# Seven block products in place of eight in a two-layer expert network, with the instruction order made by a list scheduler

## The chip, the cores and the metric

The kernel runs on one core of a Trainium2 chip. Times are device microseconds from the first to the last work of an execution. Every run is marked fast or slow; medians below name which runs they cover. "PE" is TensorE's matrix unit, "PEld" its weight load, "DVE" VectorE, "ACT" ScalarE, "POOL" GpSimd, "SP" SyncE, which here issues DMAs.

## The reference, cut to what matters

```python
# linear attention: batch 8, heads 8, seq 576, head_dim 64
q_p, k_p = phi(q), phi(k)                  # phi(x) = elu(x) + 1
kv = einsum('bhsd,bhse->bhde', k_p, v);  z = sum(k_p, over s)
x  = (q_p @ kv) / (q_p @ z + 1e-6)         # reshaped to 4608 tokens x 512
# mixture of 4 experts, all of them for every token
p = domain_probs / sum(domain_probs)
for e in range(4):
    h = maximum(x @ w1[e], 0)              # 512 -> 1024
    out += p[:, e] * (h @ w2[e])           # 1024 -> 512
```

The expert network is nearly all of the arithmetic: 4608 tokens, 4 experts, two products of 512 x 1024.

## The kernel before

It keeps all weights in SBUF as fp16 and goes through tokens in nine tiles of 512. For each tile and expert (a "unit" of 64 matmuls) it makes the first layer, ACT applies the ReLU while it moves PSUM to SBUF, then the second layer, and DVE multiplies by p and adds to a sum in SBUF. The attention of later batches is emitted between the tiles.

```python
def emit_unit(j, e):                       # 512 tokens, one expert
    for fj in range(FC):                   # 8
        for dc in range(DC):               # 4
            nc.tensor.matmul(out=ph, lhsT=w1_sb[e][:, dc, fj*P:(fj+1)*P],
                             rhs=xT_all[:, dc, j*NT:(j+1)*NT], ...)   # 512 columns
        nc.scalar.activation(ht, ph, AF.Relu)
    for ns in range(NSUB):                 # 4
        for fj in range(FC):               # 8
            nc.tensor.matmul(out=py, lhsT=hT[fj][:, ns*P:(ns+1)*P],
                             rhs=w2_sb[e][:, fj, :], ...)             # 512 columns
        nc.vector.scalar_tensor_tensor(out=acc[:, ns, :], in0=py, scalar=pscal,
                                       in1=acc[:, ns, :], op0=AO.mult, op1=AO.add)
# weights: fp32 by DMA (SP queue) into a staging tile, then a cast by DVE (w1) or ACT (w2)
# order at the start:
emit_attention_batch(0); emit_w1(0); emit_w2(0); emit_probs(); emit_w1(1)
emit_unit(0, 0); emit_attention_batch(1); emit_w2(1); emit_unit(0, 1)
# [...] weights of experts 2 and 3 between units of tiles 0 and 1, then tile after tile
```

Of the kernel before, what the change touches and what calls it, by code (L numbers as in the profile page):

```python
# [7 lines left out]


FP32 = mybir.dt.float32  # L10
# [4 lines left out]
SX = float(2.0**14)  # L15
INV = float(2.0 ** (-14))
# [3 lines left out]
def kernel(  # L20
# [10 lines left out]
    nc = tc.nc  # L31
# [6 lines left out]
    R = 96  # L38
    KC = S // R
    QC = S // (2 * R)  # L40
    HD = H * D
    DC = HD // P
    FC = F // P
    NT = 512
    NTILES = N // NT
    NSUB = NT // P
    DE = D + 1
    HG = 4
    NG = H // HG
    NCH = (S + P - 1) // P  # L50
    TAIL = S - (NCH - 1) * P
    NTP = N // P

    pconst = ctx.enter_context(tc.tile_pool(name="pconst", bufs=1))
    identh = pconst.tile([P, P], FP16, tag="identh")
    make_identity(nc, identh)
    NKV = 3
    kvs = []
    for i in range(NKV):
        kvz = pconst.tile([P, 2, DE], FP16, tag=f"kvz{i}", name=f"kvz{i}")  # L60
        nc.gpsimd.memset(kvz, 0.0)
        kvs.append(kvz)
    n_kv = [0]

    pw = ctx.enter_context(tc.tile_pool(name="pw", bufs=1))
    w1_sb = [pw.tile([P, DC, F], FP16, tag=f"w1_{e}", name=f"w1_{e}") for e in range(E)]
    w2_sb = [pw.tile([P, FC, Dm], FP16, tag=f"w2_{e}", name=f"w2_{e}") for e in range(E)]
    w1_src = moe_w1.rearrange("e (dc p) f -> e p dc f", p=P)
    w2_src = moe_w2.rearrange("e (fc p) d -> e p fc d", p=P)
    p_sb = pw.tile([P, NTP, E], FP32, tag="pnorm")  # L70

    px = ctx.enter_context(tc.tile_pool(name="px", bufs=1))
    xT_all = px.tile([P, DC, N], FP16, tag="xT")

    pa = ctx.enter_context(tc.tile_pool(name="pa", bufs=1))
    pm = ctx.enter_context(tc.tile_pool(name="pm", bufs=1))
    ppm = ctx.enter_context(tc.tile_pool(name="ppm", bufs=1, space=bass.MemoryType.PSUM))
    ppa = ctx.enter_context(tc.tile_pool(name="ppa", bufs=1, space=bass.MemoryType.PSUM))

    out_tiled = out.rearrange("(j ns p) d -> j p ns d", ns=NSUB, p=P)  # L80

    def emit_w1(e):
        FQ = F // 4
        for h4 in range(4):
            wr = pw.tile([P, DC, FQ], FP32, tag="wraw", bufs=3)
            nc.sync.dma_start(out=wr, in_=w1_src[e, :, :, h4 * FQ : (h4 + 1) * FQ])
            nc.vector.tensor_copy(w1_sb[e][:, :, h4 * FQ : (h4 + 1) * FQ], wr)

    def emit_w2(e):
        for h4 in range(4):  # L90
            wr = pw.tile([P, 2, Dm], FP32, tag="wraw", bufs=3)
            nc.sync.dma_start(out=wr, in_=w2_src[e, :, h4 * 2 : h4 * 2 + 2, :])
            nc.scalar.copy(w2_sb[e][:, h4 * 2 : h4 * 2 + 2, :], wr)  # L93

    def emit_probs():
        p_raw = pw.tile([P, NTP, E], FP32, tag="praw")
        nc.sync.dma_start(
            out=p_raw, in_=moe_domain_probs.rearrange("(nt p) e -> p nt e", p=P)
        )
        p_rsum = pw.tile([P, NTP], FP32, tag="prsum")  # L100
        nc.vector.tensor_reduce(
            out=p_rsum, in_=p_raw, axis=mybir.AxisListType.X, op=AO.add
        )
        nc.vector.tensor_scalar(p_rsum, p_rsum, 1e-9, None, AO.add)
        nc.vector.reciprocal(p_rsum, p_rsum)
        nc.vector.scalar_tensor_tensor(
            out=p_sb,
            in0=p_raw,
            scalar=INV,
            in1=p_rsum.broadcast_to([P, NTP, E]),  # L110
            op0=AO.mult,
            op1=AO.mult,
        )

    def emit_attention_batch(b):
        for g in range(NG):
            hs = slice(g * HG, (g + 1) * HG)
            kst = pa.tile([R, HG, KC, D], FP32, tag="kst", bufs=2)
            vst = pa.tile([R, HG, KC, D], FP32, tag="vst", bufs=2)
            qst = pa.tile([R, QC, HG, 2, D], FP32, tag="qst", bufs=2)  # L120
            nc.sync.dma_start(
                out=kst, in_=k[b, hs].rearrange("h (p c) d -> p h c d", p=R)
            )
            nc.sync.dma_start(
                out=vst, in_=v[b, hs].rearrange("h (p c) d -> p h c d", p=R)
            )
            q_src = q[b, hs].rearrange("h (c p r) d -> c p h r d", c=QC, r=2)
            for c in range(QC):
                nc.sync.dma_start(out=qst[:, c], in_=q_src[c])



            kp = pa.tile([R, KC, HG, D], FP16, tag="kp", bufs=2)
            kpv = kp.rearrange("p c h d -> p h c d")
            ek = pa.tile([R, HG, KC, D], FP16, tag="phie", bufs=2)
            nc.scalar.activation(ek, kst, AF.Exp)  # L136
            nc.vector.tensor_scalar(kpv, kst, 0.0, 1.0, AO.max, AO.add)
            nc.vector.tensor_tensor(out=kpv, in0=ek, in1=kpv, op=AO.min)

            vp = pa.tile([R, KC, HG, DE], FP16, tag="vp", bufs=2)  # L140
            nc.gpsimd.memset(vp[:, :, :, D:DE], 1.0 / SX)
            nc.scalar.copy(vp[:, :, :, 0:D].rearrange("p c h d -> p h c d"), vst)  # L142

            qp = pa.tile([R, QC, 2, HG, D], FP16, tag="qp", bufs=2)
            eq = pa.tile([R, QC, HG, 2, D], FP16, tag="phie", bufs=2)
            nc.scalar.activation(eq, qst, AF.Exp)  # L146
            for c in range(QC):
                qv = qp[:, c].rearrange("p r h d -> p h r d")
                nc.vector.tensor_scalar(qv, qst[:, c], 0.0, 1.0, AO.max, AO.add)
                nc.vector.tensor_tensor(out=qv, in0=eq[:, c], in1=qv, op=AO.min)  # L150

            for pr in range(HG // 2):
                h0 = pr * 2
                pair = g * (HG // 2) + pr
                psum_kv = ppa.tile([P, 2, DE], FP32, tag="aps", bufs=3)
                for c in range(KC):
                    nc.tensor.matmul(  # L157
                        out=psum_kv,
                        lhsT=kp[:, c, h0 : h0 + 2, :],
                        rhs=vp[:, c, h0 : h0 + 2, :],  # L160
                        start=(c == 0),
                        stop=(c == KC - 1),
                    )
                kvz = kvs[n_kv[0] % NKV]
                n_kv[0] += 1
                nc.scalar.copy(out=kvz[0:D, 0, :], in_=psum_kv[0:D, 0, :])
                nc.scalar.copy(out=kvz[D:P, 1, :], in_=psum_kv[D:P, 1, :])

                psum_qT = ppa.tile([P, QC, 2, R], FP16, tag="aps", bufs=3)
                for c in range(QC):  # L170
                    for r in range(2):
                        nc.tensor.transpose(  # L172
                            out=psum_qT[:, c, r, :],
                            in_=qp[:, c, r, h0 : h0 + 2, :],
                            identity=identh[0:R, 0:R],
                        )
                qT = pa.tile([P, S], FP16, tag="qTsb", bufs=2)
                nc.vector.tensor_copy(
                    out=qT, in_=psum_qT.rearrange("p c r i -> p (c r i)")
                )  # L180

                x_sb = pa.tile([P, NCH, 2, D], FP16, tag="xsb", bufs=2)
                for c0, c1 in ((0, 3), (3, NCH)):
                    psum_nd = ppa.tile([P, 3, 2, DE], FP32, tag="aps", bufs=3)
                    for c in range(c0, c1):
                        w = P if c < NCH - 1 else TAIL
                        nc.tensor.matmul(  # L187
                            out=psum_nd[0:w, c - c0],
                            lhsT=qT[:, c * P : c * P + w],
                            rhs=kvz,  # L190
                            start=True,
                            stop=True,
                        )
                    recip = pa.tile([P, 3, 2, 1], FP32, tag="recip", bufs=3)
                    for a0, a1, w in (
                        ((0, 3, P),) if c1 == 3 else ((0, 1, P), (1, 2, TAIL))
                    ):
                        nc.vector.reciprocal(
                            recip[0:w, a0:a1], psum_nd[0:w, a0:a1, :, D:DE]
                        )  # L200
# [8 lines left out]
                for c in range(NCH):  # L209
# [10 lines left out]
                    in_=psum_xT.rearrange("p (c r i) -> p c r i", c=QC, r=2),  # L220
                )

    accs = {}

    def emit_unit(j, e):
        if e == 0:
# [97 lines left out]
```

## Time and profile before

| before | value |
|---|---|
| time, median of the first 3 runs | 595.45 us |
| PE busy | 563.3 of 593.0 us |
| DVE, ACT busy | 234.2, 286.2 us |
| one group of 32 matmuls with 512 columns | 6.91 us, so 216 ns each |
| one tile of 512 tokens with a batch of attention | 62.31 us (from 188.37 to 250.68) |

The page of the kernel before: busy time of each engine, rows of the 40 slices of the span (a digit is tenths busy), and the chain of work that ended last.

```profile
span 593.0 us, 7743 instructions
PE 563.3 (95%) x3008; PEld 266.6 (45%) x3008; DVE 234.2 (39%) x516; ACT 286.2 (48%) x449; POOL 12.9 (2%) x25
...
PE   1789997999999999999999999999999999999997
...
DMA  9989889915556003800181010000100010000001
...
PE 82%; DMA 7%; ACT 6%; DVE 3%; issue 1%; SPq 0%; ACTq 0%
```

PE is busy for 70% or more of each slice from the second (a slice is 14.8 us) and for 90% or more from the eighth to the last but one, and the DMA engines are busy for 80% or more of each of the first eight slices, in which the weights and two batches arrive. From the chain in order of time (start, duration, what):

```profile
188.37 6.91 PE ph L233 x32
...
250.68 6.91 PE ph L233 x32
```

These are the first-layer matmuls of one expert in two successive tiles: 62.31 us from tile to tile. The timeline of PE around 136 us shows how narrow matmuls follow one another:

```profile
136.10 0.33 PE L211 MATMUL psum_xT<-identh,x_sb 128*128 128x128 f16 x3
...
136.38 0.45 PE L157 MATMUL psum_kv<-vp,kp 96*128 96x130 f16 x5
136.67 0.38 PE L233 MATMUL ph<-xT_all,w_3_75 128*128 128x512 f16 x1
```

Five matmuls of 130 columns, each with a weight load of its own, begin at 136.38 and the next group at 136.67: 58 ns apart. The change rests on such short matmuls.

### The profile page before, as it was taken

The page shows a single profiled execution, that of the slowest core. Times are in us where ns is not written, and L with a number is a line of the kernel's source. Part 1 is how long each engine was busy: PE and PEld are TensorE (multiplying, and loading weights), DVE is VectorE, ACT ScalarE, POOL GpSimd, SP SyncE. Part 2 cuts the span into 40 slices and gives each one's busy share as a digit, 9 for nine tenths or more (in the row PEclk, how much of TensorE's full clock was granted, in tenths as well). Part 3 has the DMA queues.
Part 4 walks back from the last instruction along what each step waited for, and adds up shares of the span by engine and source line. Part 5 has one row for each costly group of instructions (what it writes and reads, how often), then busy time and mean ns, then how long its engine had stood idle before and what let it go on. Part 6 is the DMA issues. An engine that isn't in the chain of part 4 may idle for free.

```text
span 593.0 us, 7743 instructions
## 1 busy us (share of the span) xinstructions
PE 563.3 (95%) x3008; PEld 266.6 (45%) x3008; DVE 234.2 (39%) x516; ACT 286.2 (48%) x449; POOL 12.9 (2%) x25
## 2 busy tenths in 40 slices
PE   1789997999999999999999999999999999999997
PEld 0434443445454445544454445444544444444443
DVE  3737733528466225722382228322522222222222
ACT  4476765738657334833394338333543333333332
POOL 0000000001000000000000001000000000000000
PEclk9979998999999999999999999999999999999999
DMA  9989889915556003800181010000100010000001
GB/s 214 258 255 297 236 274 273 261 28 129 183 155 156 1 0 101 211 1 1 72 197 43 1 55 19 1 0 23 50 0 2 1 72 0 1 36 35 1 1 71
DMA packets 54644, 55.09 MB, mean 93 GB/s; under 512 B 6992, under 2 KB 45904, under 8 KB 54608
## 3 DMA queue, kind: packets, MB, share of 16 engines
q1 hardware_dynamic: 54608, 54.61, 33.2%
q8 instruction: 23, 0.38, 0.3%
q14 instruction: 13, 0.11, 0.1%
HBM read 45.16 MB, written 9.44 MB: 92 GB/s over the span
## 4 chain that ended last, share of the span: by engine, by line
PE 82%; DMA 7%; ACT 6%; DVE 3%; issue 1%; SPq 0%; ACTq 0%
PE py L247 39%; PE ph L233 36%; DMA wr<-in_moe_w_dram 6%; PE psum_nd L187 2%; DMA kst<-in_k_dram 2%; PE psum_xT L211 2%; ACT ht L241 2%; PE psum_kv L157 2%; PE psum_qT L172 1%; ACT xT_all L216 1%; ACT ek L136 1%; ACT eq L146 1%; DVE x_sb L201 1%; DVE acc L258 0%; ACT w_1_77 L93 0%
## 5 line engine op out<-in xcount | busy, mean ns | idle before, releaser
L241 ACT ACTIVATE ht<-ph 128x512 f16<-128x512 f32 x288 | 168.4, 598 | 209.3 <-PE ph L233 208.9
L258 DVE SCALAR_TENSOR_TENSOR acc<-py,p_sb,acc 128x512 f32<-128x512 f32 x108 | 81.0, 750 | 263.4 <-PE py L247 263.4
L247 PEld LDWEIGHTS <-ht 128*128 128x128 f16 x1152 | 111.6, 98 | 133.3 <-issue 3.3
L233 PE MATMUL ph<-xT_all,w_0_72 128*128 128x512 f16 x288 | 78.1, 394 | 3.4 <-ACT xT_all L216 2.6
L233 PE MATMUL ph<-xT_all,w_1_73 128*128 128x512 f16 x288 | 64.9, 380 | 3.3 <-ACT ht L241 3.3
L247 PE MATMUL py<-w_0_76,ht 128*128 128x512 f16 x288 | 67.0, 379 | 0.1
L247 PE MATMUL py<-w_1_77,ht 128*128 128x512 f16 x288 | 66.6, 385 | 0.3 <-DVE acc L258 0.2
L233 PE MATMUL ph<-xT_all,w_3_75 128*128 128x512 f16 x288 | 64.9, 379 | 0.0
L247 PE MATMUL py<-w_3_79,ht 128*128 128x512 f16 x288 | 64.1, 379 | 0.0
L233 PE MATMUL ph<-xT_all,w_2_74 128*128 128x512 f16 x288 | 64.0, 379 | 0.1
L247 PE MATMUL py<-w_2_78,ht 128*128 128x512 f16 x288 | 63.7, 379 | 0.0
L233 PEld LDWEIGHTS <-w_1_73 128*128 128x128 f16 x288 | 27.9, 98 | 36.1 <-issue 3.6
L233 PEld LDWEIGHTS <-w_2_74 128*128 128x128 f16 x288 | 28.2, 98 | 34.4 <-issue 0.7
L256 DVE TENSOR_SCALAR acc<-py,p_sb 128x512 f32<-128x512 f32 x36 | 27.0, 749 | 39.0 <-PE py L247 39.0
L233 PEld LDWEIGHTS <-w_3_75 128*128 128x128 f16 x288 | 27.7, 98 | 32.6
L233 PEld LDWEIGHTS <-w_0_72 128*128 128x128 f16 x288 | 26.0, 100 | 28.2 <-issue 6.1
L201 DVE TENSOR_TENSOR x_sb<-psum_nd,recip 128x384 f16<-128x384 f32 (+2 forms) x96 | 32.7, 368 | 0.5
L157 PE MATMUL psum_kv<-vp,kp 96*128 96x130 f16 x192 | 18.9, 231 | 10.3 <-ACT vp L142 10.3
L216 ACT COPY xT_all<-psum_xT 128x576 f16<-128x576 f16 x32 | 25.7, 804 | 5.3 <-PE psum_xT L211 4.8
L146 ACT ACTIVATE eq<-qst 96x1536 f16<-96x1536 f32 x16 | 23.7, 1481 | 9.3 <-DVE qp L150 6.4
L136 ACT ACTIVATE ek<-kst 96x1536 f16<-96x1536 f32 x16 | 23.8, 1488 | 6.2 <-DMA kst<-in_k_dram 4.5
L142 ACT CAST vp<-vst 96x1536 f16<-96x1536 f32 x16 | 23.9, 1494 | 2.1 <-DMA vst<-in_v_dram 2.0
(44 smaller groups left out, 261.2 us busy)
## 6 DMA issues: line engine op xcount, KB each, us to landing
wr<-in_moe_w_dram SPq DMA_DIRECT2D x32, 512.0 KB, 5.2
kst<-in_k_dram SPq DMA_DIRECT2D x16, 576.0 KB, 5.5
vst<-in_v_dram SPq DMA_DIRECT2D x16, 576.0 KB, 6.7
qst<-in_q_dram SPq DMA_DIRECT2D x48, 192.0 KB, 5.2
out_dram<-acc SPq DMA_DIRECT2D x36, 256.0 KB, 2.0
p_raw<-in_moe_domain_probs_dram SPq DMA_DIRECT2D x1, 72.0 KB, 8.8
```

The lines of the kernel that those rows point to most:

```text
L136: nc.scalar.activation(ek, kst, AF.Exp)
L142: nc.scalar.copy(vp[:, :, :, 0:D].rearrange("p c h d -> p h c d"), vst)
L146: nc.scalar.activation(eq, qst, AF.Exp)
L157: nc.tensor.matmul(out=psum_kv, lhsT=kp[:, c, h0 : h0 + 2, :], rhs=vp[:, c, h0 : h0 + 2, :], start=(c == 0), stop=(c == KC - 1),)
L187: nc.tensor.matmul(out=psum_nd[0:w, c - c0], lhsT=qT[:, c * P : c * P + w], rhs=kvz, start=True, stop=True,)
L201: nc.vector.tensor_tensor(out=x_sb[0:w, c0 + a0 : c0 + a1], in0=psum_nd[0:w, a0:a1, :, 0:D], in1=recip[0:w, a0:a1].broadcast_to([w, a1 - a ...
L216: nc.scalar.copy(out=xT_all[:, pair, b * S : (b + 1) * S].rearrange("p (c i r) -> p c r i", c=QC, r=2), in_=psum_xT.rearrange("p (c r i) - ...
L233: nc.tensor.matmul(out=ph, lhsT=w1_sb[e][:, dc, fj * P : (fj + 1) * P], rhs=xT_all[:, dc, j * NT : (j + 1) * NT], start=(dc == 0), stop=(d ...
L241: nc.scalar.activation(ht, ph, AF.Relu)
L247: nc.tensor.matmul(out=py, lhsT=hT[fj][:, ns * P : (ns + 1) * P], rhs=w2_sb[e][:, fj, :], start=(fj == 0), stop=(fj == FC - 1),)
L256: nc.vector.tensor_scalar(acc[:, ns, :], py, pscal, None, AO.mult)
L258: nc.vector.scalar_tensor_tensor(out=acc[:, ns, :], in0=py, scalar=pscal, in1=acc[:, ns, :], op0=AO.mult, op1=AO.add,)
```

## The change

A product of two matrices cut in four blocks each needs eight block products, or seven when sums of blocks are multiplied instead (Strassen's scheme in Winograd's form). The change uses seven in both layers, except in the first layer of expert 3 and for token tile 0. The price is sums: of blocks of x and h (DVE, for each unit), of weights (DVE, once), and of results (ACT and DVE, or in PSUM by letting products accumulate). p is multiplied into x (it is never negative, so the ReLU lets it through), so that four experts can accumulate in the same PSUM banks. Weights are cast by the load itself; the Trainium skill ("DMA: Bandwidth & Descriptors", SWDGE vs HWDGE vs iDMA) says that casting loads can be issued from GpSimd only, and so they are here. Transposes of x go to the DMA engines.

The order of instructions is no longer the order of the source. Each piece is registered with a scheduler: engine, assumed duration, priority, and the names ("keys") that it reads and writes. The scheduler plays the program through once with the assumed durations and emits the instructions in the order of their planned starts; on the chip each engine runs its own list in order. In the code a "pair" is two heads of q, k and v of one batch, brought to buffers by three staging loads. Core of the diff, with cuts marked:

```diff
+class Plan:
+    HOP = 0.2
+    def add(self, eng, dur, pri, fn, r=(), w=(), move=0.0, after=0.0):
+        # [...] r: depends on the key's last writer
+        for key in w:
+            if key in self.wr:
+                deps.add(self.wr[key])          # a writer waits for the last writer
+            deps.update(x for x in self.rd.get(key, ()) if x != n)
+        # [...]
+    def order(self):
+        # [...] list scheduling; POOL keeps its source order; all DMAs share one "mover"
+            if o["move"]:
+                mover = max(done + 1.2, mover) + o["move"]
+                done = mover + 0.8
+
+    T0, TU = 84.0, 6.4
+    U = lambda n: T0 + n * TU                   # priority of unit n (256 tokens, one expert)
+
+    def load_w1(e, dcs):
+        for dc in dcs:
+            dma("POOL", 0, w1_sb[e][:, dc, :], moe_w1[e, dc * P : (dc + 1) * P, :],
+                (("w1", e, dc // 2, 0), ("w1", e, dc // 2, 1), ("w1c", e, dc)), 1.5)
+    def load_w2(e):
+        # [...]
+                (("w2", e, i, 0), ("w2", e, i, 1), ("w2c", e, c // 2)), 1.5)
+    # probs(): loads of domain_probs on SP, sums, reciprocal, product on DVE, priority 24
+
+    # first layer, experts 0 to 2: 7 products of 8 matmuls with 128 columns
+    steps = (
+        (A, ka, w1x[e][:, 2], X(2), xT[:, 1, 2:4], t_, True),
+        (Bk, kb, w1x[e][:, 1], X(1), xT[:, 0, 0:2], t_, True),
+        (W, kw, w1x[e][:, 0], X(0), xs[:, 4], x_(0), False),
+        # [...] four more; ACT and DVE combine the three banks into h
+    # second layer: 7 products of 4 matmuls with 256 columns
+    seq = (P2, P4, P1, P5, P6, P7, P3)
+
+    load_pair(0, 0, "SP", 0)
+    load_rest(0, "SP", 1)                       # last 64 tokens of batch 0
+    probs()
+    # [...] POOL, in this order: pairs and weights of the start
+    load_w2(0); load_w1(1, range(DC)); load_w2(1)
+    # [...] expert 0 of tile 0
+    load_pair(1, 0, "POOL", 0); load_rest(1, "POOL", 0)
+    load_w1(2, range(DC))
+    rest_maps(1, True, 47)                      # last 64 tokens of batch 1
+    attention(1, 0, True, 47, 0.8)
+    load_pair(1, 1, "POOL", 0); load_w2(2)
+    # [...] pairs 2 and 3 of batch 1, between them the weights of expert 3
+    for e in range(1, E):                       # tile 0, plain
+        ht = first_l1(e, 21 + 14 * e, 0.22, False)
+        first_l2(e, ht, 28 + 14 * e, 0.9, e == E - 1)
+        # [...] sums of blocks of the weights
+    # [...] 64 units, with the attention of batches 2 to 7
+        for o in pl.order():
+            o["fn"]()
```

## The prediction

> **What bounds it now.** TensorE. The page gives PE 563.3 us of a 593.0 us span, and the chain of waits is 82% PE (second-layer matmuls 39%, first-layer 36%), 7% DMA, 6% ACT. In the timeline a group of 32 matmuls with 512 columns follows the next after 6.91 us: 216 ns each, at full clock. There are 36 x 64 = 2304 of them, 497.5 us. DVE (234) and ACT (286) have slack. In the first 105 us the DMA engines are 80 to 100% busy at about 260 GB/s, and PE loses 30 us.
>
> **What changes.** Token tile 0 stays plain (55 us), made while the weights arrive. The other 4096 tokens go in 64 units of 256 tokens (tile, half, expert).
> - Second layer: 7 products of 4 matmuls with 256 columns. Scaling 512 columns/216 ns gives about 109 ns each: 28 x 109 = 3.05 us (plain 3.46).
> - First layer, experts 0 to 2: 7 products of 8 matmuls with 128 columns, each with its own weight load. In the timeline, runs of 128- and 130-column matmuls with 128-column loads start 56 to 57 ns apart (five in 0.45 us, one lasting 0.22), so the loads hide: 56 x 56 = 3.14 us. The Trainium skill ("TensorE: Matmul & The Clock Gate", Back-to-back issue gap) says about 81 ns sustained; the trace's short runs disagree. Expert 3 stays plain, 3.48 us.
> - PE per unit: 6.19 us seven, 6.53 plain; 48 and 16 of them: 402 us. The attention of batches 2 to 7 adds 24 pairs x 10 matmuls x 57 ns = 14 us. PE floor from unit 0 on: 416 us.
>
> **What it adds elsewhere.** DVE loses the 750 ns accumulations, but gets sums. With 412 ns per 512 fp16 elements in SBUF (measured) and about 0.7 us for an fp32 PSUM source of 512 (750 ns measured with a scalar): 1.1 input sums + 2.1 combinations + 1.65 hidden sums per seven unit, 2.4 closing sums per four units; about 4.6 us per unit, and 1.8 more while attention runs: 6.4 of about 6.6 us. ACT: about 5.3 us. Transposes move to DMA, two units ahead, and should hide. DVE becomes the second limit, and the chain PSUM, ACT, PSUM, DVE inside a unit leaves a few tenths of slack in three banks. I allow 0.3 us of PE wait per unit, 19 us.
>
> **Start.** Weights 16.8 MB and two batches 7.1 MB must land before tile 0 ends. Weight packets of 2 KB took a median 86 ns, an estimated 380 GB/s; 1.5 KB ones 250. Estimate: 75 to 92 us, so units start near 86 us.
>
> **Sum.** 86 + 416 + 19 = 521; a tail of 7 us, less 6 that units overlap with the start: 522 us. About 70 us less, mostly from one eighth fewer multiplications, the rest from fewer small PE instructions, transposes off PE, a shorter start.
>
> **What would show it.** First-layer seven-product matmuls start 56 ns apart; PE over 92% in the middle; DVE about 75 to 90% busy, ACT about 75%; a unit takes 6.5 to 6.9 us; chain mostly PE; DMA transposes land in under 6 us, waited for by nobody.
>
> **What would make it wrong.** 81 ns in the first layer (+67 us: all gain gone); combining instructions over 0.8 us, making DVE the bound; in-order queues, laid out with assumed durations, waiting on late work; casting loads far below 260 GB/s; a lower clock.

## The result, and the profile after

The change is faster, by about half of what was predicted: 561.33 us (median of 4 fast runs, 559.94 to 562.97) against 595.17 us. The ratio is 0.9449, with a 95% interval from 0.9414 to 0.9485. Ratios in this document are the mean time of one kernel's fast runs over that of the other's fast runs of the same rounds, so not quite the ratio of the medians quoted.

The page of the changed kernel, with the same lines (a slice is 14.0 us here):

```profile
span 561.2 us, 13887 instructions
PE 498.4 (89%) x5624; PEld 427.8 (76%) x5624; DVE 413.5 (74%) x993; ACT 335.7 (60%) x617; POOL 38.9 (7%) x62
...
PE   0067979578999999999999999999999999999994
...
DMA  9999328398535745693668447564434242523211
...
PE 83%; DVE 6%; DMA 6%; ACT 2%; issue 2%; POOL 1%; DVEq 0%; ACTq 0%; POOLq 0%
```

From the eleventh slice to the last but one PE is busy for 90% or more, as before. The holes are in the first ten, and the DMA row has a hole there as well (3, 2 in the fifth and sixth slices), in the middle of the weight loads. The chain in order of time has the plain first layer of expert 3 once in four units; two of its pieces in the middle and two at the end, then a run of first-layer products and one of second-layer products:

```profile
182.63 0.87 PE l1b L705 x8
...
393.88 0.87 PE l1b L705 x8
...
496.92 0.87 PE l1b L705 x8
499.97 0.89 PE l1b L649 x16
500.87 0.87 PE l2b L757 x8
...
547.12 0.87 PE l1b L705 x8
549.74 2.63 PE l2b L757 x24
```

Sixteen 128-column matmuls take 0.89 us, 56 ns each; eight of 256 columns 0.87 us, 109 ns each. The timeline shows how the two layers alternate on PE:

```profile
308.83 0.61 PE L649 MATMUL l1b<-xs,w 128*128 128x128 f16 x8
309.28 0.60 PE L757 MATMUL l2b<-t,s 128*128 128x256 f16 x4
309.72 0.61 PE L649 MATMUL l1b<-xs,w 128*128 128x128 f16 x8
```

Thirty-two units take 393.88 - 182.63 = 211.25 us, 6.60 each, while attention runs beside them, and the eight from 496.92 to 547.12 take 50.20 us, 6.28 each. The prediction's sums for PE alone were (48 x 6.19 + 16 x 6.53) / 64 = 6.28 without attention and 14 / 48 = 0.29 more with it, 6.57. The steady part therefore runs at the predicted floor, almost without PE waits.

The table of stretches for the changed kernel shows the same (stretch and its length; busy time and number of instructions of PE, weight load, DVE, ACT, POOL; granted clock; DMA share; GB/s):

```profile
0.00:28.00 28.00, 0.80 (x6) 0.48 (x7) 6.78 (x21) 6.11 (x9) 17.75 (x31) 1.00 1.09 229
28.00:56.00 28.00, 19.67 (x97) 10.17 (x97) 17.30 (x51) 10.67 (x25) 14.81 (x22) 0.95 1.16 224
56.00:84.00 28.00, 23.94 (x117) 10.96 (x116) 17.91 (x31) 11.41 (x21) 5.42 (x8) 0.99 0.30 73
84.00:112.00 28.00, 20.09 (x108) 9.54 (x107) 19.41 (x46) 14.69 (x30) 0.93 (x2) 0.87 0.59 127
112.00:140.00 28.00, 22.83 (x173) 13.27 (x174) 17.24 (x49) 23.92 (x45) 0.00 (x0) 0.90 0.83 190
140.00:340.00 200.00, 197.88 (x2487) 184.53 (x2485) 173.46 (x420) 138.86 (x259) 0.00 (x0) 1.00 0.59 132
```

In the first 140 us PE is busy 87.3 us, some of it at a lowered clock. From 140 to 340 us it is busy 197.88 of 200 us, with DVE at 87% and ACT at 69%.

So the account is this. The second layer of the last unit ends at 549.74 + 2.63 = 552.4 us. Taking off the 416 us of PE work that the 64 units and six batches need leaves 136 us for the start, where 86, less 6 of overlap, was predicted. The terms are now 136 + 416 + 9 us of closing sums and stores = 561. The first unit product itself, predicted near 86 us, begins at 125.56:

```profile
125.56 1.05 PE L649 MATMUL l1b<-xT,w1x 128*128 128x128 f16 x16
```

Against the kernel before, eight tiles at their steady price became cheaper by 67 us: six with attention went from 62.31 to 8 x 6.60 = 52.8 us, two without from 55.3 (eight groups of 6.91) to 50.2. The rest (start, tile 0, tail) went from 593.0 - 484.4 = 108.6 to 561.2 - 417.2 = 144.0 us. The start gave back 35.4 us of the 67.

Two waits stand out in the start. The timeline of DVE (start, duration, ..., in brackets the idle time before it and what ended it):

```profile
9.29 0.43 DVE L325 TENSOR_TENSOR kqp<-ek,kqp 128x512 f16<-128x512 f16 x1 [0.23 <-ACT ek L332]
24.95 0.29 DVE L265 TENSOR_REDUCE prs<-praw 128x32 f32<-128x128 f32 x1 [15.23 <-DMA praw<-in_moe_domain_probs_dram]
...
26.28 0.68 DVE L289 TENSOR_SCALAR kqpr<-kqr 64x1024 f16<-64x1024 f32 x1
```

DVE holds still for 15.23 us for p, which nobody needs before 61 us, and the map of the last 64 tokens that the first attention needs stands behind it. And the timeline of POOL:

```profile
52.79 1.21 POOL L219 DMA_DIRECT2D w<-in_moe_w_dram  x2
78.58 0.72 POOL L219 DMA_DIRECT2D kq<-in_k_dram  x1 [24.57 <-DVE kqp L325]
...
80.94 3.99 POOL L219 DMA_DIRECT2D w<-in_moe_w_dram  x6
```

The last six weight loads of expert 3 wait 24.57 us behind a staging load of batch 1, whose buffer DVE frees at 78 us: that is the hole in the DMA row.

PE itself waits for something else. Of the 52.7 us that it stands idle in the first 140, the three longest sums are these (who waited for whom, us in total, times, longest):

```profile
PE l2b L345 <- DVE kqpr L290: 19.2, 2, 17.4
PE l2b L342 <- DVE kqp L325: 11.7, 3, 9.8
PE at L388 <- DVE x L401: 9.4, 10, 1.8
```

The others are for DVE and ACT too; behind the 17.4 us stands DVE's wait for p. None of PE's own waits in that stretch is put down to a load, and a weight load ended 0.3 us of waiting on PE's weight-load side.

### What the kernel's own plan says

The scheduler runs when the program is built. Printing its planned starts (this is no measurement) gave:

```
planned end                                                   563.7 us
planned issue of weight loads on POOL   22.2 22.9 28.1 28.8 34.0 34.7 39.9 40.6 ... 126.75
planned first product of unit 0                               121.7 us
```

The plan itself ends at 563.7 us. In it, weight loads come in pairs, at first 5.9 us from one pair to the next, and the last lands at 135 us; on the chip, while nothing else was in the way, one was issued every 1.3 us (six from 19.68 to 26.32 us). The reason can be read in the diff: the loads of chunk dc = 0 and dc = 1 of w1 both name the key ("w1", e, 0, .) as written, and w2 likewise, so the bookkeeping makes the second wait for the landing of the first, though they fill different bytes. On the chip there is no such wait: those six went out 1.3 us apart, though a load took 8.9 us (median) to land. But PE, ACT and DVE go through lists made for late weights. Setting the trace beside the plan, PE instruction by PE instruction, gives how far the chip was behind it:

| trace at | 50 us | 70 us | 90 us | 110 us | 140 us | 530 us |
|---|---|---|---|---|---|---|
| changed kernel, us behind its plan | 16.3 | 14.4 | 7.6 | 4.4 | 1.6 | -3.2 |

### The profile page after: what moved, and what is told of

Read it like the earlier page. It is cut to its first block, busy times and chain, and to the rows that moved or that the text cites. A ratio compares the mean times of both kernels' runs of the same rounds, so it can differ in the third digit from the quotient of the medians.

```text
span 561.2 us, 13887 instructions
## 1 busy us (share of the span) xinstructions
PE 498.4 (89%) x5624; PEld 427.8 (76%) x5624; DVE 413.5 (74%) x993; ACT 335.7 (60%) x617; POOL 38.9 (7%) x62
## 4 chain that ended last, share of the span: by engine, by line
PE 83%; DVE 6%; DMA 6%; ACT 2%; issue 2%; POOL 1%; DVEq 0%; ACTq 0%; POOLq 0%
PE l2b L757 33%; PE l1b L649 25%; PE l1b L705 10%; PE l1b L495 6%; DMA w<-in_moe_w_dram 5%; PE l2b L505 3%; PE at L388 2%; PE at L364 1%; DVE x L401 1%; DVE ot L562 1%; DMA xT<-xp 1%; PE l2b L495 1%; DVE rc L399 1%; DVE kqp L324 1%; DVE kqp L325 0%
## 5 line engine op out<-in xcount | busy, mean ns | idle before, releaser
L649 PE MATMUL l1b<-xs,w 128*128 128x128 f16 x1536 | 114.8, 219 | 1.5 <-ACT h L686 0.9
L757 PE MATMUL l2b<-w,h 128*128 128x256 f16 x768 | 112.3, 273 | 0.8 <-DVE h L693 0.8
L757 PE MATMUL l2b<-t,s 128*128 128x256 f16 x768 | 111.1, 273 | 0.0
L649 PEld LDWEIGHTS <-w 128*128 128x128 f16 x1536 | 99.6, 98 | 5.4 <-issue 1.8
L757 PEld LDWEIGHTS <-s 128*128 128x128 f16 x1024 | 93.6, 98 | 8.1
L607 ACT ACTIVATE xp<-x,p_nat 128x512 f16<-128x512 f16 x112 | 75.2, 716 | 7.5 <-DMA xT<-xp 7.2
L649 PEld LDWEIGHTS <-w1x 128*128 128x128 f16 x1152 | 74.9, 98 | 4.6 <-issue 2.0
L757 PEld LDWEIGHTS <-h 128*128 128x128 f16 x768 | 69.9, 98 | 7.1 <-DVE h L693 1.1
L705 PE MATMUL l1b<-xT,w 128*128 128x256 f16 x512 | 74.2, 273 | 0.0
L724 ACT ACTIVATE h<-l1b 128x512 f16<-128x512 f32 x64 | 38.2, 596 | 43.2 <-PE l1b L705 35.6
L705 PEld LDWEIGHTS <-w 128*128 128x128 f16 x512 | 49.6, 98 | 5.6
L683 ACT ACTIVATE h<-l1b 128x512 f16<-128x512 f32 x48 | 28.6, 596 | 33.7 <-PE l1b L649 33.3
```

Of the source, the lines that this page charges most:

```text
L607: pl.add("ACT", 0.65, pri, lambda c=c, src=src, ps=ps: nc.scalar.activation(xp[:, c, :], src, AF.Copy, scale=ps), r=r, w=(("xp", xi, c),))
L649: nc.tensor.matmul(out=bank[:, fc * P : (fc + 1) * P], lhsT=wt[:, kc, fc * P : (fc + 1) * P], rhs=r[:, kc, :], start=(start and fc == 0 an ...
L705: nc.tensor.matmul(out=ph[:, f2 * 2 * P : (f2 + 1) * 2 * P], lhsT=w1_sb[e][:, dc, (2 * fp + f2) * P : (2 * fp + f2 + 1) * P], rhs=xT[:, :, ...
L724: lambda ph=ph, f=f, c0=c0: nc.scalar.activation(h[:, :, f, c0 : c0 + 2, :], ph.rearrange("p (c u t) -> p u c t", c=2, u=2), AF.Relu), r=( ...
L757: nc.tensor.matmul(out=l2b[bank][:, half * HD : (half + 1) * HD], lhsT=a[:, c, :], rhs=w[:, c], start=(opens and first and c == 0), stop=( ...
```

## The experiments

Four explanations were set against each other. **P**: the start is as long as it is because every queue was laid out for weights that the plan lets arrive too late. **Q**: weight loads are held in POOL's queue behind staging loads. **R**: DVE's 15 us for p are what is lost. **D**: the casting loads are too slow.

### e1_keys: the false chain removed from the bookkeeping

```diff
-                (("w1", e, dc // 2, 0), ("w1", e, dc // 2, 1), ("w1c", e, dc)), 1.5)
+                (("w1c", e, dc),), 1.5, co=(("w1", e, dc // 2, 0), ("w1", e, dc // 2, 1)))
 # w2 likewise; Plan.add keeps a set of writers per key, and a writer named in co=
 # joins the set without waiting for the others
```

> Edit: in the scheduler's bookkeeping two weight loads that fill one quadrant no longer wait for each other (they write different bytes); the instructions are the same, only their order changes. Theory P (the start is slow because every queue was laid out for weights that the plan lets arrive too late, plan end 563.7 us): the new plan ends at 532 us, first unit product at 102 us instead of 122, so I expect 530 to 542 us, and the steady part unchanged at about 6.45 us per unit. Rival Q (a weight load blocked in POOL's queue behind staging loads): the order on POOL is the same, so over 550. Rival R (the late domain_probs load that holds DVE until 25 us): it is still there, so over 550. Rival D (DMA rate of casting loads): over 555.

Measured: 548.94, 549.74 and 547.33 us in three fast runs; ratio to before 0.926 (0.9232 to 0.9287). The profiled run was an outlier of 1345.53 us and gives no usable trace. The new order alone saves 12 us, with the instructions unchanged and POOL's list in its old order, so D as the whole cause is out, and Q and R as the whole cause narrowly (both said over 550). But P's number, 530 to 542, was missed by 6 us or more: something else was lost as well.

### e2_probs: the work on p planned later

```diff
-    pl.add("DVE", 0.6, 24, lambda: go(...), r=("praw",), w=("pnat",))
+    pl.add("DVE", 0.6, 24, lambda: go(...), r=("praw",), w=("pnat",), after=36.0)
 # and the same for p_rest
```

> Edit: the two groups of DVE instructions that normalise p are planned not before 36 us, so DVE no longer waits for the p load before the first attention. Rival R (that 15 us wait is what the start loses): 545 to 550 us. Theory P: the plan runs 16 us ahead of the engines at 45 us but only 1.2 us ahead at 140 us, so the 15 us are swallowed later anyway: 557 to 561 us.

Measured: 555.77 us (553.91 to 556.29), ratio 0.9374 (0.935 to 0.9397). This is between the two: of the 15 us, about 7 show at 30 us (then the load of the last 64 tokens, landed at 19.7, holds the first attention) and 5 to 6 reach the end. R is a part of the cause, not the whole of it. P's view that slack in the old plan swallows all of the 15 us was too strong.

### e3_wfirst: the weights taken out of the queue's block

```diff
+        early = [o for o in pool[29:] if o["move"] == 1.5]   # w1, w2 of experts 2 and 3
+        for o in order:
+            if o is pool[26]:                                # first staging load of batch 1
+                for x in early: x["fn"]()
+            if id(o) not in moved: o["fn"]()
```

> Edit: plan and order of all engines unchanged, but the 14 to 16 weight loads of experts 2 and 3 are issued on POOL ahead of the staging loads of batch 1, so the 24.6 us block at 54 to 79 us cannot hold them. Rival Q: 545 to 551 us. Theory P: PE, ACT and DVE still follow the old order; 556 to 563 us.

Measured: 561.94 us (560.52 to 562.79), ratio 0.9488: nothing gained. POOL's timeline in this run, at the first and the last of the weight loads and the first staging load behind them:

```profile
24.66 0.72 POOL L219 DMA_DIRECT2D w<-in_moe_w_dram  x1 [0.57 <-DMA w<-in_moe_w_dram]
...
48.58 0.72 POOL L219 DMA_DIRECT2D w<-in_moe_w_dram  x1 [0.60 <-DMA w<-in_moe_w_dram]
50.09 0.73 POOL L219 DMA_DIRECT2D kq<-in_k_dram  x1 [0.80 <-DVE rc L399]
```

All weights are issued by 49 us, each released by the landing of an earlier one, 18 loads with 17 gaps in 23.92 us: 1.41 us for 512 KB of source, an estimated 373 GB/s. Thirty-five microseconds less for the last weights (issued by 49 instead of 85 us) change nothing at the end. The edit has a price that could hide a gain: the first staging load of batch 1 goes out at 50.09 instead of 30.69 us. But the last staging loads, which the attention of batch 1 ends with, go out at 75.98 instead of 78.58, and PE is 2.7 us further in its list at 140 us than in the changed kernel, so no large gain was lost that way. This is the sharpest result of the first four: the weights were not what PE waited for; its list was.

### e4_plain1: no seven-product first layer

```diff
-    SEVEN1 = (0, 1, 2)
+    SEVEN1 = ()
```

> Edit: first layer plain for all four experts (no seven-product first layer; second layer as changed). If PE sets the pace and 128-column matmuls go out every 56 ns, each of 48 units costs 32 x 109 = 3.49 instead of 56 x 56 = 3.14 us of PE, +0.34: 561 + 16.5 = 574 to 580 us, with DVE far less busy. If they went out every 81 ns (sustained figure of the skill) the edit would save 49 us instead; if DVE set the pace it would save time too.

Measured: 576.57 us (573.82 to 578.46), ratio 0.9727 (0.9689 to 0.9765). That is 14 to 15 us more than the changed kernel (561.33, and 562.51 in e10), with DVE busy 108.53 us instead of 173.46 in the stretch from 140 to 340 us. PE sets the pace, and the seven-product first layer earns nearly what the instruction count says. (The 81 ns of the expectation is the figure that the prediction cites with its page.) The stretch in this run:

```profile
140.00:340.00 200.00, 200.00 (x1895) 179.95 (x1894) 108.53 (x268) 138.42 (x254) 0.00 (x0) 1.00 0.54 124
```

### e5_keys_again: a trace for the mended bookkeeping

> The same kernel as e1_keys once more, because the profiled run of e1 was an outlier (1345 us[...]) and gives no usable trace. Theory P': the new plan ends at 532 us, and the about 15 us by which the late domain_probs load sets everything back at 25 us are no longer swallowed, since the new plan has less slack: 532 + 15 = 547, as the three undisturbed runs of e1 say (547 to 550). In the trace PE should run 13 to 16 us behind the plan both at 50 us and at 300 us. Rival D (weights land too late for the tighter order): the distance is small at 50 us and grows between 60 and 110 us.

Measured: 545.65 and 549.66 us. The trace runs 15.0 us behind its plan at 50 us, 16.0 at 110, 13.2 at 300 and 10.7 at 530 us. P' is P with the delay by p added to it. The delay is there at 50 us and doesn't grow between 60 and 110, as P' said and D denied. DVE still waits for p:

```profile
23.51 0.29 DVE L266 TENSOR_REDUCE prs<-praw 128x32 f32<-128x128 f32 x1 [13.98 <-DMA praw<-in_moe_domain_probs_dram]
```

This explains e1's miss: a tighter plan has less slack, so an early delay is carried to the end.

### e6_keys_probs: both edits

> Both edits: weight loads of one quadrant not chained in the plan, and the p normalisation planned after 36 us. Plan end 532.1 us. Theory P': PE starts the first attention at 21.5 us as in e2, about 7 us behind the plan, and keeps that distance: 537 to 542 us, 7 to 11 less than e1. If the two gains were not additive (rival: something else holds the start once the keys are mended): 545 to 550.

Measured: 539.66 us (538.98 to 544.01), ratio 0.9094 (0.9056 to 0.9132), in the expected range. The distance to the plan was not quite as said: 11.1 us at 50 us, 14.0 at 130, 9.4 at 500. Together the edits give about 22 us, more than e1's 12 and e2's 5.5 added up.

### e7_keys_probs_rest: the last 64 tokens loaded first

```diff
-    load_pair(0, 0, "SP", 0)
-    load_rest(0, "SP", 1)
+    load_rest(0, "SP", 0)
+    load_pair(0, 0, "SP", 1)
```

> As e6, and the three loads of the last 64 tokens of batch 0 (128 KB each, landed at 19 us in e2) are issued before the first head pair. Plan end 531.6 us. Theory P': the first attention matmul on these rows moves from 21.5 us to about 14 us, and 4 to 7 us of it reach the end: 531 to 537 us. If the start is by then held by DMA rate: no gain over e6, within 2 us.

Measured: 536.39 us (534.33 to 536.96), ratio 0.9031 (0.8995 to 0.9067). The first attention matmul on PE begins at 15.04 us instead of 21.68 in e2 (the first line is e2, the second e7):

```profile
21.68 0.62 PE L364 MATMUL at<-vp,kqp 128*128 128x130 f16 x4
15.04 0.59 PE L365 MATMUL at<-vp,kqp 128*128 128x130 f16 x4 [15.04 <-ACT vp L329]
```

About 3 us reach the end, less than the 4 to 7 expected, though the median lies in the range given.

### e8_dve_double: is DVE a second limit?

```diff
+            if i == 2:                       # the third hidden sum once more, same result
+                pl.add("DVE", 0.42, U(n + 1) + d - 0.5, ...)
```

> The changed kernel with one hidden sum (DVE, 128x512 fp16, 0.42 us) done twice in each of the 64 units: 27 us more DVE work, the same result. If DVE is off the critical path with real slack (PE 99% busy from 140 to 450 us): 561 to 566 us (plan end 566.1 against 563.7). If DVE already co-limits, as the prediction allowed for (19 us of PE waits): 572 to 590 us.

Measured: 565.16 us (562.51 to 566.98), ratio 0.9518 (0.9473 to 0.9564). Sixty-four more DVE instructions of 0.42 us, 27 us of work, cost 2.7 to 3.8 us (against 562.51 and 561.33), no more than the scatter of the runs. PE was busy 198.21 us of the 200 from 140 to 340:

```profile
140.00:340.00 200.00, 198.21 (x2483) 183.99 (x2483) 179.90 (x443) 136.87 (x256) 0.00 (x0) 1.00 0.57 127
```

(The plan of this kernel, built again, ends at 573.4 us and not at 566.1 as the expectation says.) DVE does not hold the changed kernel back; where it would begin to was not tried.

### e9_start_earlier and e10_changed_again

```diff
-    T0, TU = 84.0, 6.4
+    T0, TU = 74.0, 6.4
-    rest_maps(1, True, 47); attention(1, 0..3, True, 47 / 56 / 65 / 72, 0.8)
+    rest_maps(1, True, 34); attention(1, 0..3, True, 34 / 42 / 50 / 57, 0.8)
 # on top of e7
```

> As e7, and the attention of batch 1 is given priorities 13 to 15 us earlier (34, 42, 50, 57 instead of 47, 56, 65, 72; T0 74), nothing else. Plan end 522.5 us, first unit product at 90 us instead of 100. Theory P' (the start is as long as the laid-out order makes it; about 5 to 7 us behind the plan): 526 to 532 us, 5 to 9 less than e7. Rival D (by now the DMA engines hold the start, 90% busy until 56 us): within 2 us of e7, 534 to 538.

> The changed kernel without an edit, on the same chip as e9, as the base for it: 558 to 563 us.

Measured on the same chip: e9 525.95 us (525.11 to 527.24), ratio 0.8878 (0.8847 to 0.891); the unedited change 562.51 us (558.8 to 565.67), ratio 0.9494. e9 beats both kernels: 11.2% less than before, 36.6 us less than the change as it came, by the order of instructions alone. The stretches of e9, in the order of columns as above:

```profile
0.00:28.00 28.00, 8.42 (x48) 4.95 (x49) 13.78 (x43) 11.56 (x21) 16.04 (x29) 1.00 1.04 218
28.00:56.00 28.00, 24.38 (x103) 11.04 (x102) 19.67 (x48) 10.59 (x21) 16.99 (x25) 1.00 1.16 229
56.00:84.00 28.00, 28.00 (x168) 14.21 (x166) 22.86 (x52) 17.85 (x37) 5.43 (x8) 1.00 0.85 196
84.00:112.00 28.00, 27.81 (x254) 18.64 (x254) 21.74 (x51) 23.40 (x45) 0.00 (x0) 1.00 0.76 177
112.00:140.00 28.00, 28.00 (x358) 26.27 (x356) 24.70 (x62) 20.20 (x38) 0.00 (x0) 1.00 0.59 135
140.00:340.00 200.00, 199.62 (x2511) 186.58 (x2510) 177.23 (x442) 148.00 (x276) 0.00 (x0) 1.00 0.63 141
```

PE is full from 56 us on, and the granted clock stays at 1.00, where the changed kernel had 0.87 and 0.90 from 84 to 140 us. Its plan ends at 522.5 us. From its page:

```profile
PE 493.1 (94%) x5624; PEld 426.8 (81%) x5624; DVE 410.8 (78%) x993; ACT 334.2 (64%) x617; POOL 38.5 (7%) x62
```

With the same 5624 matmuls PE is busy 5.3 us less than in the changed kernel (498.4) and idle 31.1 us less (31.7 of 524.8 against 62.8 of 561.2): the gain is waiting that went.

## Why the prediction was right or wrong

**The bound: right.** PE holds 82% of the chain before and 83% after, and doubling a DVE sum (e8) cost about an eighth of its own duration.

**The cost of the products: right.** 56 ns for 128-column matmuls with a weight load each, and 109 ns for 256 columns, were predicted from short runs and estimated by scaling; the chain after shows 0.89 us for sixteen and 0.87 us for eight. The Trainium skill's sustained 81 ns ("TensorE: Matmul & The Clock Gate", Back-to-back issue gap) did not come: the first layer, in runs of 8 to 24 matmuls between those of the second, kept 56 ns for hundreds of microseconds. Averaged with the 256-column ones between them, it is 75 ns for each matmul and weight load (84 in a unit of 6.28 us); a long unbroken stream of 128-column matmuls was not run. e4 confirms the count by its cost of about 15 us.

**The costs on DVE and ACT: right.** 420 ns for a 512-element fp16 sum and 687 ns where PSUM is a source, against 412 and about 700 foreseen. The Trainium skill ("VectorE: DVE Perf Modes", The perf-mode tier table) gives tensor_tensor two elements per cycle for 16-bit operands in SBUF and one when PSUM is involved, and the trace agrees with that: 1024 fp16 elements in SBUF (L445, a sum of weights) took 684 ns, as long as 512 from PSUM (687). DVE at 87% from 140 to 340 us lies in the predicted 75 to 90%; ACT at 69% is a little under the predicted 75%.

**"I allow 0.3 us of PE wait per unit, 19 us": wrong, too much.** PE waited about 2 us in the 200 from 140 to 340. The scheduler had put the other layer's products between those of the first (the timeline at 309 us), so PE had work while the chain PSUM, ACT, PSUM, DVE ran.

**"Transposes land in under 6 us, waited for by nobody": nearly right.** They landed in 3.3 us (median); ACT waited 8.1 us and DVE 3.7 us for them in total, and PE stayed full.

**"Estimate: 75 to 92 us, so units start near 86 us": wrong, and this is the step that failed.** The estimate was DMA volume over DMA rate, and that part was not too short: in e3 all weights were issued by 49 us. What failed was to take the arrival of the data as what sets the start. The list order does: the first unit product came at 125.56 us, and PE had waited for DVE and ACT, not for weights. The lists were made for weights that arrive at up to 135 us, because two loads that share a key were chained in the plan; that alone is worth about 12 us (e1), the rest of the order about 24. In the prediction's sum, the units start as if at 136 us, where 86 less 6 of overlap was put, 56 us late; 19 us of waiting that did not come, and a tail of 9 us for 7, leave the 39 us of the miss. The prediction did name "in-order queues, laid out with assumed durations, waiting on late work" among its risks, but gave it no time. The numbers to see it were in the diff: keys, the 1.2 and 0.8 us around each transfer, and 16 chained pairs.

**What closes the gap, one run after the other:** bookkeeping mended, about 12 us (e1); p later, about 9 more (e6); last 64 tokens first, about 3 (e7); earlier priorities for batch 1, about 10 (e9). The parts are not independent: p later is worth 5.5 us in the old order. e9 ends 4 us above the predicted 522, which is luck in part: its first unit product begins at 97.57 us and not at 86, and the 19 us of waits that were allowed for didn't come.

**What stays open.** The runs show that the order, with the instructions and transfers unchanged, is worth 36 us. How much of that is the lowered clock in the start was not tested by itself. Two numbers bound it: PE's busy time fell by only 5.3 us from the changed kernel to e9, and of e9's four runs the two with the lower mean clock (0.983 and 0.987) were the faster ones (525.11 and 525.30 us, against 526.59 and 527.24 at 0.997). Where more DVE work would begin to bind, and whether a fourth seven-product first layer would pay, was not tried.

## What to carry to other kernels

When a kernel orders its own instructions by a plan, the plan is part of its performance: check it for waits that the chip will not have (two writers of one name), and compare its times with the trace engine by engine. An in-order queue turns one wrongly placed instruction into idle time for all that stands behind it (15.23 us on DVE, 24.57 us on POOL), and data that arrived earlier than planned gained nothing here (e3). Predict the start of a kernel from the lists and not from transfer volume alone.

## What the Trainium skill lacked or had wrong

- "TensorE: Matmul & The Clock Gate", Back-to-back issue gap: about 81 ns sustained for 128-column matmuls with weight loads; here 56 ns (sixteen in 0.89 us) in runs of 8 to 24 between 256-column ones, all through the steady part, 75 ns on average over both kinds. An unbroken stream was not measured.
- "DMA: Bandwidth & Descriptors": it says who may issue a casting load, but I found no rate for one. Here an fp32-to-fp16 load of 512 KB of source was issued every 1.41 us in a row of 18 (e3), an estimated 373 GB/s of source.
- The same page: no figure for a small load of small rows among large ones. The 64 KB load of domain_probs took 20.5 us from issue to landing while the weight loads took 8.9 us (median), and it cost DVE 15.23 us.
- No page that I read describes a whole run like e1's outlier: with a recorded granted clock of 1.00, the run took 1345.53 us where the same kernel took 546 to 550, and PE's mean 256-column matmul of the second layer took 538 ns where the changed kernel had 273, while DVE's hidden sums (419 ns) and ACT's ReLUs (597 ns) took as long as there. Its cause is open; it came once in 43 runs of the changed and edited kernels.
